# Until the MoE begins: ScalarE's roundings one step later, weight conversion dealt by a table, two buffers for v

## The chip, the cores and the metric

The kernel runs on one core of a Trainium2 chip. The metric is the device time of one execution in microseconds, the median of several runs. The engines are TensorE (PE, matmuls; its weight loads are PEld), VectorE (DVE), ScalarE (ACT), GpSimd (POOL) and the queue of SyncE (SP), which issues nearly all the transfers.

## The reference

Attention with rotary embedding (4 batches, 8 heads, 576 positions, 64 per head), then a feed-forward part that this kernel's names call the MoE, whose hidden layer is gated by a convolution over three neighbouring positions. All of it is float32; the weights come as float64.

```python
q_rot, k_rot = (rotate(q), rotate(k))
scores = scale * np.matmul(q_rot, k_rot.transpose(0, 1, 3, 2))
attn = np.exp(scores - np.max(scores, axis=-1, keepdims=True))
attn = attn / (np.sum(attn, axis=-1, keepdims=True) + 1e-09)
x = np.matmul(attn, v)                  # heads side by side: 576 x 512
h = np.maximum(x @ w_in, 0.0)           # 512 -> 1024
conv_out[s] = sum(conv_w[k] * h[s + k - 1] for k in range(3))
out = (h * sigmoid(conv_out)) @ w_out   # 1024 -> 512
```

## The kernel before

Two heads of a batch make a pair p (16 pairs), and each pair takes five steps: four of 128 query rows for both heads, and a fifth for the remaining 64 rows of both. Step n = 5p + s is thus the unit of the plan. A step holds, for its rows: the scores S (line 260, and line 286 for the last 64 keys), their negated row maximum on VectorE (line 268), the exponential on ScalarE (line 272, into tiles st, or str for a pair's fifth step), and one step later the turning T of the result on TensorE (line 320) and its copy to pt by ScalarE (line 198). Five steps after its first, a pair's pt is multiplied with v (E, line 388; x's half j = 0 and half j = 1). ScalarE copies the product to xn (line 398), VectorE multiplies it with the reciprocal sums that came back by a transfer (line 402, `norm`), ScalarE rounds it to xT (line 406) and GpSimd subtracts the rounded from the exact value (line 407), so that matmuls get x as a high and a low part.

q and k come by six transfers each (lines 148 to 150), GpSimd applies the rotary tables (`rope`: six instructions of line 189 and three of line 192 for a part), and VectorE turns them (line 233 for q, lines 236 to 242 for k). v comes by four transfers into the tiles vm and vr (`load_v`, lines 160 and 161).

For the first 26 steps (`WIDE = 26`) there is no MoE work. In them the 16 weight pieces, 128x512 each, are converted from float64: per piece a transfer (line 587), `first` on ScalarE (line 549), `mid` on VectorE (lines 552, 558 and 561), `third` on VectorE (line 566, which gives wf), and then `split`: ScalarE rounds wf (line 609), and GpSimd subtracts in four quarters (line 612). From step 26 the MoE's units go into the steps: M1 (line 421), its relu on ScalarE into the four tiles rr (line 429), the convolution on VectorE (lines 433 and 435), tanh, gate, rounding, GpSimd's subtraction (line 453) and M2 (lines 503 and 523). The borders of the rr tiles are set to zero by GpSimd (lines 740 and 741) as step 26 begins.

The order on every engine is that in which the code emits. `at(n, rank, fn)` puts a piece of work into step n, in order of rank: 0 T, 0.2 row maxima, 0.3 exponentials, 0.35 the copies that `after` postponed, 0.4 conversion, 0.45 turning of q and k, 0.5 the next step's S, 1.7 and 2.7 `norm`, 2 and 4 further matmuls, 4.5 reciprocals and their transfers, 18 `rope`, 19 loads. `defer(k, fn)` runs fn some ticks later, mostly within the same step. The 48 conversion units are spread evenly over steps 0 to 24.

## Time and profile before

| | us |
|---|---|
| median of 3 runs | 501.51 |
| the runs | 499.65, 501.51, 502.05 |
| the profiled execution, its own time | 499.73 |
| its span, first to last instruction | 497.9 |
| lies around the span | 1.8 |

The trace is read by stretches: the steps without MoE work up to about 123 us, a transition from there to about 187 us, and the rest, in which TensorE carries both attention and MoE. Times are from the span's start. The step of an instruction is found by counting row maxima on VectorE: two in each of a pair's first four steps, one in the fifth.

### The profile page before, as it was taken

The page shows a single profiled execution, that of the slowest core. Times are in us where ns is not written, and L with a number is a line of the kernel's source. Part 1 is how long each engine was busy: PE and PEld are TensorE (multiplying, and loading weights), DVE is VectorE, ACT ScalarE, POOL GpSimd, SP SyncE. Part 2 cuts the span into 40 slices and gives each one's busy share as a digit, 9 for nine tenths or more (in the row PEclk, how much of TensorE's full clock was granted, in tenths as well). Part 3 has the DMA queues.
Part 4 walks back from the last instruction along what each step waited for, and adds up shares of the span by engine and source line. Part 5 has one row for each costly group of instructions (what it writes and reads, how often), then busy time and mean ns, then how long its engine had stood idle before and what let it go on. Part 6 is the DMA issues. An engine that isn't in the chain of part 4 may idle for free.

```text
span 497.9 us, 12391 instructions
## 1 busy us (share of the span) xinstructions
PE 459.4 (92%) x4572; PEld 361.2 (73%) x4572; DVE 357.4 (72%) x643; ACT 327.0 (66%) x927; POOL 300.2 (60%) x479
## 2 busy tenths in 40 slices
PE   1979877787979999999999999999999999999997
PEld 1445554454666869787978787979797978899886
DVE  5689888998394978786868687777674665567921
ACT  2578878777583958686868686868686763234510
POOL 3599997999947666747584849393921213233510
PEclk9989899998897999999999999999999999999999
DMA  8975955755330707070807090707110200100011
GB/s 221 176 137 146 230 129 144 196 113 107 74 69 27 120 9 150 18 149 12 155 19 149 14 153 13 143 25 129 38 48 25 61 12 25 43 22 22 0 65 42
DMA packets 140559, 42.71 MB, mean 86 GB/s; under 512 B 132156, under 2 KB 135252, under 8 KB 140500
## 3 DMA queue, kind: packets, MB, share of 16 engines
q1 hardware_dynamic: 139156, 41.54, 39.9%
q8 instruction: 36, 0.59, 0.5%
q10 hardware_dynamic: 1344, 0.39, 0.4%
q14 instruction: 23, 0.19, 0.1%
HBM read 37.12 MB, written 4.79 MB: 84 GB/s over the span
## 4 chain that ended last, share of the span: by engine, by line
PE 65%; DVE 13%; POOL 7%; DMA 4%; SPq 4%; ACT 3%; issue 2%; DVEq 0%; POOLq 0%; ACTq 0%
PE pm L421 12%; PE sp L260 11%; PE pm L523 10%; PE mt L503 10%; PE pm L388 9%; PE mt L421 7%; PE tp L320 5%; DVE negm L268 4%; POOL rq L189 2%; DMA rq<-q 2%; POOL rk L189 2%; POOL rq L192 2%; DVE wt L558 1%; SPq L149 1%; DVE wt L552 1%
## 5 line engine op out<-in xcount | busy, mean ns | idle before, releaser
L268 DVE TENSOR_REDUCE negm<-sp 128x1 f32<-128x576 f32 x144 | 102.4, 748 | 37.1 <-PE sp L260 28.9
L272 ACT ACTIVATE st<-sp,negm 128x576 f32<-128x576 f32 x128 | 93.8, 740 | 36.7 <-DVE negm L268 35.7
L260 PE MATMUL sp<-kT,qT 64*128 64x288 f32 (+4 forms) x556 | 101.0, 468 | 3.6 <-DVE kT L236 1.6
L453 POOL TENSOR_TENSOR g<-c,g 128x288 fp32r<-128x288 f32 (+4 forms) x88 | 52.5, 618 | 84.6 <-ACT g L452 84.3
L198 ACT ACTIVATE pt<-tp 128x512 f32<-128x512 f32 (+3 forms) x176 | 84.0, 530 | 2.1 <-PE tp L320 1.6
L435 DVE SCALAR_TENSOR_TENSOR c<-rr,cw,c 128x288 f32<-128x288 f32 x128 | 78.4, 612 | 4.5
L421 PE MATMUL pm<-xT,winh 128*128 128x290 f32 x352 | 74.5, 306 | 0.0
L189 POOL TENSOR_TENSOR rq<-rq,tabt 128x192 f32<-128x192 f32 x90 | 58.9, 687 | 16.2 <-DMA rq<-q 16.1
L260 PEld LDWEIGHTS sp<-kT,qT 64*128 64x128 f32 (+1 forms) x556 | 47.5, 178 | 24.8 <-issue 11.1
L407 POOL TENSOR_TENSOR xT<-xn,xT 128x290 fp32r<-128x290 f32 x32 | 27.9, 876 | 61.3 <-ACT xT L406 61.2
L320 PEld LDWEIGHTS tp<-idf,st 64*128 64x128 f32 x1024 | 43.1, 140 | 28.6 <-ACT st L272 18.6
L320 PE MATMUL tp<-idf,st 64*128 64x64 f32 x1024 | 49.4, 229 | 12.7 <-ACT st L272 12.7
L189 POOL TENSOR_TENSOR rk<-rk,tabt 128x192 f32<-128x192 f32 x90 | 57.1, 667 | 5.6 <-DMA rk<-k 5.6
L421 PEld LDWEIGHTS pm<-xT,winh 128*128 128x128 f32 x352 | 56.2, 189 | 1.8
L523 PE MATMUL pm<-wouth,g 64*128 64x256 f32 x576 | 55.5, 282 | 0.0
L388 PE MATMUL pm<-pt,vm 128*64 128x290 f32 x368 | 52.6, 424 | 2.2 <-DMA vm<-v 2.0
L421 PE MATMUL pm<-xT,winl 128*128 128x290 f32 x176 | 52.0, 295 | 0.0
L523 PEld LDWEIGHTS pm<-wouth,g 64*128 64x128 f32 x576 | 48.5, 185 | 0.0
L523 PE MATMUL pm<-woutl,g 64*128 64x256 f32 x288 | 44.0, 277 | 0.0
L433 DVE TENSOR_SCALAR c<-rr,cw 128x288 f32<-128x288 f32 x64 | 28.0, 437 | 21.7 <-ACT rr L429 20.5
L444 DVE SCALAR_TENSOR_TENSOR c<-c,rr 128x288 f32<-128x288 f32 x64 | 35.2, 572 | 9.4 <-ACT c L441 9.4
L388 PEld LDWEIGHTS pm<-pt,vm 128*64 128x64 f32 x368 | 27.2, 142 | 20.1 <-ACT pt L198 2.4
(108 smaller groups left out, 876.6 us busy)
## 6 DMA issues: line engine op xcount, KB each, us to landing
rq<-q SPq DMA_DIRECT2D x30, 144.0 KB
rq<-q SPq DMA_DIRECT2D x60, 72.0 KB
rk<-k SPq DMA_DIRECT2D x30, 144.0 KB
rk<-k SPq DMA_DIRECT2D x60, 72.0 KB
w<-moe_w_in SPq DMA_DIRECT2D x8, 512.0 KB
vm<-v SPq DMA_DIRECT2D x32, 128.0 KB
w<-moe_w_out SPq DMA_DIRECT2D x8, 512.0 KB
rb<-rd SPq DMA_DIRECT2D x16, 144.0 KB
```

Of the source, the lines that this page charges most:

```text
L189: nc.gpsimd.tensor_tensor(out=y, in0=y, in1=tabt[:, a:a + 3], op=ALU.mult)
L198: nc.scalar.activation(out=out, in_=in_, func=AF.Copy, scale=1.0 if sc is None else sc)
L260: nc.tensor.matmul(out=out, lhsT=qt[64 * h:64 * h + 64, c], rhs=kt[64 * h:64 * h + 64, a:a + n], start=True, stop=True)
L268: reds.setdefault((p, s), []).append(lambda: nc.vector.tensor_reduce(out=nm, in_=sc, axis=AX.XY if len(sc.shape) == 3 else AX.X, op=ALU.ma ...
L272: lambda: nc.scalar.activation(out=dst, in_=sc, func=AF.Exp, bias=nm, scale=1.0, accum_out=sm)
L320: nc.tensor.transpose(ps[r][:, 64 * k:64 * k + 64], x[i], idf[i, i])
L388: nc.tensor.matmul(out=xp[64 * h:64 * h + 64, :], lhsT=vmain[p][:, h, i, :] if i < 4 else vrem[:, h, :], rhs=pt[:, 2 * i + h if i < 4 else ...
L421: nc.tensor.matmul(out=ps[:, 0:XW], lhsT=w[:, kk, fs], rhs=xT[:, xs, e, :], start=(i == 0), stop=(i == n - 1))
L435: nc.vector.scalar_tensor_tensor(out=c, in0=r[:, j + e:j + e + HS], scalar=cw[:, 8 * e + f:8 * e + f + 1], in1=c, op0=ALU.mult, op1=ALU.add,)
L453: nc.gpsimd.tensor_tensor(out=lo, in0=c[:, o:o + n], in1=hi.bitcast(F32), op=ALU.subtract)
L503: nc.tensor.matmul(out=ops[tt][:, 0:width], lhsT=g_tile(tt, f, e), rhs=w[:, f, cols], start=(f == 0 and i == 0), stop=(f == NF - 1 and i = ...
L523: nc.tensor.matmul(out=ps[r][:, 0:256], lhsT=g_tile(tt, f, e)[rows], rhs=w[rows, f, cols], start=(f == 0 and i == 0), stop=(f == NF - 1 an ...
```

## The change

There are four edits.

- x's rounding (lines 406 and 407). Before, it ran a tick after `norm`. Now, as long as the next step is below 26, it stands in the next step at rank 0.37: behind that step's exponentials and postponed copies.
- The rounding of a weight piece (lines 609 and 612). Before, it ran two ticks after `third`; now it stands in the next step at rank 0.38.
- The dealing of conversion. Before, equal numbers of units per step; now by the table `ROOM`, one weight for each of a pair's five steps: 1.5, 1.8, 2.5, 0.8, 2.6. The last piece's `mid` moves from step 23 to step 24.
- v. vm and vr have two buffers each, and `load_v(p)` stands in the pair's second step everywhere (before: the fourth, from step 25 on the third). One more memset of vr comes with it, on VectorE in step 6.

```diff
-    vrem = keep.tile([128, 2, D], F32, name="vr")
+    vrem = [keep.tile([128, 2, D], F32, name=f"vr_{s}") for s in range(2)]
...
-        if p == 0:
-            nc.vector.memset(vrem, 0.0)
+        if p < 2:
+            nc.vector.memset(vrem[p], 0.0)
...
-        t = vmain[p] = p1.tile([128, 2, 4, D], F32, tag="vm", name="vm")
+        t = vmain[p] = p1.tile([128, 2, 4, D], F32, tag="vm", name="vm", bufs=2)
...
-        norms[p, j] = lambda: (norm(), defer(1, split))
+        def both():
+            norm()
+            if late["n"] + 1 < WIDE:
+                at(late["n"] + 1, 0.37, split)
+            else:
+                defer(1, split)
+
+        norms[p, j] = both
...
-            defer(2, split)
+            at(late["n"] + 1, 0.38, split)
...
+    ROOM = (1.5, 1.8, 2.5, 0.8, 2.6)
...
-                at(n + (2 if n >= WIDE - 1 else 3), 19, lambda p=p: load_v(p))
+                at(n + 1, 19, lambda p=p: load_v(p))
...
-            nw = len(wsteps)
+            room = [ROOM[x % STEPS] for x in range(WIDE - 1)]
+            ends = [sum(room[:x + 1]) / sum(room) for x in range(WIDE - 1)]
             for i, u in enumerate(wsteps):
-                x = (WIDE - 1) * i // nw
-                at(x, 0.4, u)
+                at(next(x for x, e in enumerate(ends) if (i + 0.5) / len(wsteps) <= e), 0.4, u)
```

VectorE in steps 23 and 24, before. The row maxima x2 are step 23's, the single one is step 24's; w_1345 is the last weight piece, and the xn rows are `norm` of x's two halves:

```order
L268 TENSOR_REDUCE negm<-sp 128x1 x2
L566 SCALAR_TENSOR_TENSOR wf<-w_1235,wt 128x512
L552 TENSOR_SCALAR wt<-wt 128x512
L558 TENSOR_SCALAR wt<-wt 128x512
L561 SCALAR_TENSOR_TENSOR wt<-w_1345,wt 128x512
L236 STREAM_TRANSPOSE kT<-rk 128x576
L240 STREAM_TRANSPOSE kr_89<-rk 64x64 x2
L242 STREAM_TRANSPOSE kT<-rk 128x64
L402 TENSOR_TENSOR xn<-xn,rb 128x290
L268 TENSOR_REDUCE negm<-sp 128x1
L566 SCALAR_TENSOR_TENSOR wf<-w_1345,wt 128x512
L402 TENSOR_TENSOR xn<-xn,rb 128x290
```

The same place after the change, from step 23's turning of k on; w_1295 and w_1349 are the last two pieces:

```order
L236 STREAM_TRANSPOSE kT<-rk 128x576
L240 STREAM_TRANSPOSE kr_90<-rk 64x64 x2
L242 STREAM_TRANSPOSE kT<-rk 128x64
L402 TENSOR_TENSOR xn<-xn,rb 128x290
L268 TENSOR_REDUCE negm<-sp 128x1
L573 SCALAR_TENSOR_TENSOR wf<-w_1295,wt 128x512
L559 TENSOR_SCALAR wt<-wt 128x512
L565 TENSOR_SCALAR wt<-wt 128x512
L568 SCALAR_TENSOR_TENSOR wt<-w_1349,wt 128x512
L573 SCALAR_TENSOR_TENSOR wf<-w_1349,wt 128x512
L402 TENSOR_TENSOR xn<-xn,rb 128x290
L268 TENSOR_REDUCE negm<-sp 128x1 x2
```

The `third` of the last piece but one and the `mid` of the last moved from ahead of step 24's row maximum to behind it, and all five stand now between it and step 25's pair of row maxima.

ScalarE from step 24 to the copy of E's first half (`xn<-tp`), before; str is step 24's exponential, st x2 are step 25's:

```order
L406 ACTIVATE xT<-xn 128x290
L198 ACTIVATE pt<-tp 128x8x64 x2
L272 ACTIVATE str_82,sums<-sp,negm 128x576
L198 ACTIVATE pt<-sp 128x128
L398 ACTIVATE xn<-sp 128x145
L198 ACTIVATE pt<-tp 128x5x64
L198 ACTIVATE pt<-tp 128x4x64
L198 ACTIVATE pt<-tp 64x64
L609 ACTIVATE wouth<-wf 128x512
L272 ACTIVATE st,sums<-sp,negm 128x576 x2
L198 ACTIVATE pt<-sp 128x128
L398 ACTIVATE xn<-tp 128x290
```

And after the change:

```order
L272 ACTIVATE str_83,sums<-sp,negm 128x576
L198 ACTIVATE pt<-sp 128x128
L398 ACTIVATE xn<-sp 128x145
L406 ACTIVATE xT<-xn 128x290
L198 ACTIVATE pt<-tp 128x5x64
L198 ACTIVATE pt<-tp 128x4x64
L198 ACTIVATE pt<-tp 64x64
L272 ACTIVATE st,sums<-sp,negm 128x576 x2
L198 ACTIVATE pt<-sp 128x128
L406 ACTIVATE xT<-xn 128x290
L616 ACTIVATE wouth<-wf 128x512 x2
L398 ACTIVATE xn<-tp 128x290
```

x's rounding went from ahead of step 24's exponential to behind the copy to xn, and x's other half and two weight roundings stand now ahead of the copy of E's first half.

GpSimd from the fifth pair's subtraction of x to the zeroing of the rr borders, before (rk and rq are `rope` of the next pairs):

```order
L189 TENSOR_TENSOR rk<-rk,tabt 128x192 x6
L192 TENSOR_TENSOR rk<-rk 128x6x32 x3
L612 TENSOR_TENSOR woutl<-wf,wouth 128x128 x12
L407 TENSOR_TENSOR xT<-xn,xT 128x290
L189 TENSOR_TENSOR rq<-rq,tabt 128x192 x6
L192 TENSOR_TENSOR rq<-rq 128x6x32 x3
L612 TENSOR_TENSOR woutl<-wf,wouth 128x128 x4
L407 TENSOR_TENSOR xT<-xn,xT 128x290
L189 TENSOR_TENSOR rk<-rk,tabt 128x192 x6
L192 TENSOR_TENSOR rk<-rk 128x6x32 x3
L740 MEMSET rr_1716 128x1
```

And after the change:

```order
L189 TENSOR_TENSOR rk<-rk,tabt 128x192 x6
L192 TENSOR_TENSOR rk<-rk 128x6x32 x3
L619 TENSOR_TENSOR woutl<-wf,wouth 128x128 x8
L407 TENSOR_TENSOR xT<-xn,xT 128x290
L189 TENSOR_TENSOR rq<-rq,tabt 128x192 x6
L192 TENSOR_TENSOR rq<-rq 128x6x32 x3
L407 TENSOR_TENSOR xT<-xn,xT 128x290
L619 TENSOR_TENSOR woutl<-wf,wouth 128x128 x8
L189 TENSOR_TENSOR rk<-rk,tabt 128x192 x6
L192 TENSOR_TENSOR rk<-rk 128x6x32 x3
L747 MEMSET rr_1718 128x1
```

A weight piece's four quarters moved from ahead of `rope` of q to behind it; ahead of the first rk row and ahead of the memset both orders hold the same work.

## Rows read from the trace of the kernel before

**Rows 1.** The page's first line: the span and all instructions.
```profile
span 497.9 us, 12391 instructions
```

**Rows 2.** Busy time by engine in two stretches; columns as the first line says.
```profile
core 0: us, PE busy (x) PEld busy (x) DVE busy (x) ACT busy (x) POOL busy (x), PEclk, DMA share, GB/s
18.00:123.00 105.00, 84.06 (x867) 52.38 (x867) 94.49 (x153) 83.16 (x217) 100.01 (x157) 0.95 0.70 153
...
186.80:498.00 311.20, 307.43 (x3153) 261.04 (x3150) 211.50 (x394) 196.49 (x576) 150.60 (x235) 1.00 0.29 61
```

**Rows 3.** VectorE's waits from 18 to 123.2: total us, times, longest us.
```profile
DVE xn L402 <- ACT xn L398: 3.7, 3, 1.3
DVE wt L552 <- ACT wt L549: 1.5, 1, 1.5
...
DVE kT L236 <- POOL rk L192: 1.0, 1, 1.0
DVE qT L233 <- POOL rq L192: 1.0, 2, 0.5
```

**Rows 4.** GpSimd's waits from 17 to 137, all there are.
```profile
POOL rq L189 <- DMA rq<-q: 7.3, 2, 6.8
POOL xT L407 <- ACT xT L406: 2.7, 1, 2.7
POOL woutl L612 <- ACT wouth L609: 1.8, 1, 1.8
```

**Rows 5.** Timeline of VectorE, steps 23 and 24: start, us, instruction, idle before.
```profile
115.13 0.83 DVE L566 SCALAR_TENSOR_TENSOR wf<-w,wt 128x512 int32<-128x512 int32 x1
...
118.08 0.77 DVE L236 STREAM_TRANSPOSE kT<-rk 128x576 f32<-128x576 f32 x1
...
119.96 0.74 DVE L268 TENSOR_REDUCE negm<-sp 128x1 f32<-128x576 f32 x1
```

**Rows 6.** Timeline of GpSimd from 114: the last ropes and weight quarters.
```profile
114.29 2.13 POOL L192 TENSOR_TENSOR rk<-rk 128x192 f32<-128x192 f32 x3
116.38 6.50 POOL L612 TENSOR_TENSOR woutl<-wf,wouth 128x128 fp32r<-128x128 f32 x12
...
128.74 1.71 POOL L612 TENSOR_TENSOR woutl<-wf,wouth 128x128 fp32r<-128x128 f32 x4
...
136.10 0.10 POOL L740 MEMSET rr<- 128x1 f32 x1
```

**Rows 7.** Timeline of ScalarE, steps 24 to 26.
```profile
120.13 0.45 ACT L406 ACTIVATE xT<-xn 128x290 fp32r<-128x290 f32 x1 [2.41 <-DVE xn L402]
...
123.86 0.63 ACT L609 ACTIVATE wouth<-wf 128x512 fp32r<-128x512 f32 x1
...
127.75 0.41 ACT L398 ACTIVATE xn<-tp 128x290 f32<-128x290 f32 x1 [1.48 <-POOL rq L192]
```

**Rows 8.** Timeline of TensorE: step 26's scores, and E in step 30.
```profile
127.56 1.29 PE L260 MATMUL sp<-kT,qT 64*128 64x288 f32 x8
...
149.37 4.16 PE L388 MATMUL pm<-pt,vm 128*64 128x290 f32 x15 [2.04 <-DMA vm<-v]
```

**Rows 9.** Timeline of VectorE, steps 27 and 28.
```profile
136.34 0.36 DVE L433 TENSOR_SCALAR c<-rr,cw 128x288 f32<-128x288 f32 x1
136.74 1.07 DVE L435 SCALAR_TENSOR_TENSOR c<-rr,cw,c 128x288 f32<-128x288 f32 x2
138.55 1.42 DVE L268 TENSOR_REDUCE negm<-sp 128x1 f32<-128x576 f32 x2 [0.74 <-PE sp L260]
```

**Rows 10.** Busy time in three stretches of E on TensorE, columns as in Rows 2.
```profile
123.40:127.60 4.20, 4.20 (x22) 1.87 (x22) 2.00 (x5) 2.76 (x8) 4.20 (x8) 0.60 0.33 51
131.10:133.80 2.70, 2.70 (x23) 1.41 (x22) 0.00 (x0) 1.40 (x5) 2.70 (x6) 1.00 0.60 115
149.40:155.00 5.60, 5.60 (x23) 3.38 (x25) 1.97 (x3) 0.93 (x4) 5.60 (x10) 0.50 0.03 7
```

**Rows 11.** Timeline of SP's queue, first issue of rk's six and of vm's.
```profile
143.38 0.31 SPq L148 DMA_DIRECT2D rk<-k  x1
...
146.49 0.44 SPq L160 DMA_DIRECT2D vm<-v  x1
```

More of the change, by code (lines that the diff above doesn't have):

```diff
@@ L154, in load_v @@
     def load_v(p):
-        if p == 0:
-            nc.vector.memset(vrem, 0.0)
+        if p < 2:
+            nc.vector.memset(vrem[p], 0.0)
         b, hp = divmod(p, NPB)
-        t = vmain[p] = p1.tile([128, 2, 4, D], F32, tag="vm", name="vm")
+        t = vmain[p] = p1.tile([128, 2, 4, D], F32, tag="vm", name="vm", bufs=2)
         for h in range(2):
             nc.sync.dma_start(out=t[:, h], in_=v[b, 2 * hp + h, 0:512, :].rearrange("(t p) d -> p t d", p=128))
-            nc.sync.dma_start(out=vrem[64 * h:64 * h + 64, h, :], in_=v[b, 2 * hp + h, 512:S, :])
+            nc.sync.dma_start(out=vrem[p % 2][64 * h:64 * h + 64, h, :], in_=v[b, 2 * hp + h, 512:S, :])
     def rope0(part, eng):
@@ L389, in emit_E @@
                     out=xp[64 * h:64 * h + 64, :],
-                    lhsT=vmain[p][:, h, i, :] if i < 4 else vrem[:, h, :],
+                    lhsT=vmain[p][:, h, i, :] if i < 4 else vrem[p % 2][:, h, :],
                     rhs=pt[:, 2 * i + h if i < 4 else 8, o + a:o + a + n],
```

## The prediction

> **What bounds the kernel now.** I read the stretches first. From 186.8 us on TensorE is busy 307.4 of 311.2 us [rows 2], so what another engine saves there is worth nothing; the change can only act by letting that stretch begin earlier. Between 18 and 123 us GpSimd is busy 100.0 and VectorE 94.5 of 105 us, TensorE 84.1 and ScalarE 83.2 [rows 2]: the steps without MoE work are paced by GpSimd and VectorE together. Next I read what these two wait for. VectorE's waits there are few [rows 3]: three times for ScalarE's copy to xn (3.7 us), once for the `first` of the small convolution weights (1.5), twice for q's rope and once for k's (1.0 each). The last belongs to step 3, where GpSimd has worked without a break since its first q landed; nothing changes ahead of that, so it stays. GpSimd waits 5.0 us in all, leaving out its start (7.3 less 6.8, then 2.7 and 1.8) [rows 4]. Last I read steps 23 to 28, where the one regime passes into the other [rows 5 to 10].
>
> **The two anchors.** The end of step 24's row maximum, at 119.96 + 0.74 = 120.70 us, I call A. Behind it the exponential, the turning, E's first half and step 26's scores (127.56) follow each other, and then TensorE's work. The second anchor is step 28's row maximum at 138.55. VectorE reaches it after TensorE's scores, with 0.74 us to spare [rows 9], or after the convolution, which needs the rr borders that GpSimd zeroes at 136.10, behind all its ropes and weight quarters [rows 6]. From 138.55 on nothing in the change alters an order that I see bind, so what 138.55 gains, the end gains.
>
> **Roundings a step later.** No instruction is added. What goes is ScalarE standing still in front of a rounding whose input VectorE has not yet made, 2.41 us in the worst case [rows 7], with the exponential and the copy to xn queued behind; that is what VectorE's three waits for xn come from. Two of them lie ahead of A: 3.7 - 1.3 = 2.4 us. The conversion now dealt to steps 9 and 14 covers them too, and step 12's wait of 1.5 us gets a piece's `mid` and `third` in front of it. q's rope loses a weight piece's quarters ahead of it, so its 1.0 us goes. That is 4.9 us. In step 19 the table leaves VectorE only one `third` between the row maximum and `norm`, so a wait for xn can come up there: nothing to 1.3 us, the longest seen; I take 0.5, since ScalarE no longer stands still first. The added memset of vr has no row of its own; it lies between 0.1 us (a memset on GpSimd, rows 6) and 0.36 (the shortest VectorE row here, rows 9); I take 0.15.
>
> **The table's dealing.** It moves no work off VectorE, but the `third` and `mid` from 115.13 to 118.08 (2.95 us) go behind A [rows 5], where VectorE waits for TensorE anyway. On VectorE alone A would come 2.95 + 4.9 - 0.65 = 7.2 us earlier.
>
> **GpSimd doesn't let it.** The turning of k in step 23 (118.08) needs k's rope, which ended at 114.29 + 2.13 = 116.42, only 1.66 us before. Ahead of that rope the new order holds exactly the same work, so it can come earlier only by waits that GpSimd loses: 2.7 + 1.8 = 4.5 us (the 0.5 for a transfer stays). Against that, two prices. x's subtraction stands ahead of q's rope as before, but its rounding is now behind an exponential and two copies on ScalarE; four such places, each nothing to about 1.3 us (the longest wait for xn, which stems from the same piece of ScalarE's queue, rows 3), so 0 to 5.2; I take 0.8, since where GpSimd runs behind, the rounding is done in time. And GpSimd is slower beside a busy VectorE: a quarter took 6.50 / 12 = 0.54 us at 116.38 with VectorE full, and 1.71 / 4 = 0.43 at 128.74 with it idle [rows 6]. A fifth of 4.9 us of VectorE's waits filled is 1.0 us. So the rope comes 4.5 - 0.8 - 1.0 = 2.7 us earlier, at 113.7, and the turning with it: 118.08 - 113.7 = 4.4. This is less than 7.2, so A gains 4.4 us, set by GpSimd.
>
> The Trainium skill ("SBUF — State Buffer", Who interferes with whom) says that a VectorE instruction with two SBUF inputs contends with a GpSimd instruction that reads SBUF, and that the one that starts second is held for the other's whole length. That speaks against filling VectorE's pauses: by the 0.54 and 0.43 the trace agrees in kind and puts the price at a fifth, and the rule at its full length is the first rival below.
>
> **What the transition takes back.** Behind A VectorE has now five conversion instructions before step 25's row maxima, 2.95 us and one `third` (0.83). Step 26's scores reuse score banks that step 25's exponentials read, so they may come later: 0 to 0.5 us, I take 0.2. On ScalarE two weight roundings (0.63 each, rows 7) stand in front of the copy of E's first half, which frees the bank that step 26's MoE matmuls take; before, that copy followed E directly at 127.75. 0 to 1.3 us; I take 0.6, the part that the exponential's delay doesn't hide. So 4.4 - 0.8 = 3.6 us reach TensorE. The other path into 138.55 gives nearly the same: borders zeroed at 136.10 - 2.7 = 133.4, 0.1 for the memset, then 1.47 for the convolution (136.34 to 137.81), so 134.97 and a gain of at most 3.6.
>
> **v.** In the first steps the loads of v move ahead of q's in SP's queue, but q's load waits there for VectorE's turning, and rope comes later still: nothing. E in step 30 waits 2.04 us for v [rows 8]. Its transfers go out at 146.49 behind k's (143.38), which wait for the turning of step 28 [rows 11]; the new order still has k's six issues ahead of v's four, so I cost this edit at nothing. Weight loads stand later in SP's queue, behind the reciprocals' transfers at steps 15 to 17; each is still issued before ScalarE's `first` takes it, by a step at the least, and ScalarE has 21.8 us free in the 105 [rows 2].
>
> **The sum.** 3.6 us off the profiled execution's 499.73 (its span 497.9 [rows 1] and 1.8 around it) is 496.1. That execution lies 1.8 below the median of the runs shown, so I forecast 501.51 - 3.6 = 497.9.
>
> **The rivals.**
>
> *GpSimd's end does not move.* If every pause that VectorE fills is lost to GpSimd, more than the 4.5 it could save, the rope ends at 116.4 as before. VectorE can then gain 1.66 us at A, and the zeroed borders at 136.2 + 1.47 = 137.67 leave 138.55 - 137.67 = 0.9 us: 500.6. For it: GpSimd was busy in all but 5 us. Against: a quarter is slowed by a fifth, not wholly. This is the skill's lock taken in full.
>
> *The transition loses more than the steps gain (slower).* TensorE's clock falls after standing still: after its 2.04 us wait at 149.37, E's 23 matmuls took 5.60 us at a granted 0.50 (1.2 GHz) where 23 took 2.70 at 1.00 (2.4 GHz) [rows 8, 10]. Before the change E's first half in step 25 ran at 0.60, and step 26's scores followed at once. Now these scores wait for step 25's exponentials, behind VectorE's five conversion instructions. If TensorE stands still there, the matmuls from 127.56 to 133.80, 6.2 us, can run at the lower level: up to 6.2 us more, and 3.4 if about half of them do. With 0.8 for the roundings and only the first rival's 0.9 gained that is 501.51 + 3.4 + 0.8 - 0.9 = 504.8. It decides from the point where A gains less than the 4.2 us that the transition loses. Against: E at 0.60 leaves little room to stand still.
>
> *v's wait goes too.* If the second buffer does free step 30, its 2.04 us go, and E's 23 matmuls run at 2.70 instead of 5.60: 2.0 + 2.9 = 4.9 more, 493.0. Only the queue's order speaks on it, and against.
>
> **How the numbers follow.** The forecast has 0.55, with 495.5 to 499.7 as its own range (a gain of 1.8 to 6: A unbound by GpSimd and no loss in the transition at one end, 2.5 of the waits taken back at the other). GpSimd's end unmoved 0.27, the slower case 0.12, v 0.06. The range 495.3 to 502.4 holds forecast and first rival with a run's spread of about 1.2 either way, and leaves out most of the other two. A measurement of this kernel can tell about 0.5%, 2.5 us, from no change. Faster by more: 0.50 of the forecast and all of v, 0.56. Slower by more: 0.10 of the slower case. Within: 0.27 and what is left of those two, 0.34.
>
> **What would show it.** In the profile after: ScalarE's waits for xn and wf before its roundings gone; VectorE's waits for xn down to one, in step 19; no wait of q's turning for rope; GpSimd's pauses before 123 us under 2 us; k's turning of step 23 starting with its rope's end, near 113.7; A near 116.3; step 28's row maximum near 135, held by the convolution or the scores; v's wait in step 30 unchanged at about 2 us. Wrong: k's turning well after its rope (then VectorE paces), GpSimd's borders still at 136, TensorE at 0.50 between steps 26 and 28, or a wait of ScalarE's `first` for a weight's transfer.

## The result, and the profile after the change

The changed kernel takes 504.37 us (median of 9 executions, 501.42 to 505.43); the kernel before, on the same chip, 500.95 (9 executions, 499.65 to 502.05). The ratio is 1.0055, with a 95% interval of 1.0036 to 1.0075: slower, by about the half per cent that can just be told. The forecast was 497.9, with a range that ended at 502.4. The nine executions fall into two groups, four at 501.4 to 502.5 and five at 504.4 to 505.4 us; the profiled one, 502.03 with a span of 500.3, is of the first, and what sets the second apart came out in the experiments. Medians and counts below are of all executions; ratios and their intervals leave out those that count as slow, over 1.5% above the fastest of the same kernel, some of the long ones of question 3 among them.

First the stretch up to 123 us, by busy time, as in [rows 2] (columns: the stretch, its length, then busy us and instructions of PE, PEld, DVE, ACT and POOL, TensorE's granted clock, DMA share, GB/s). The second row is the stretch of step 26, on which more below:

```profile
18.00:123.00 105.00, 85.16 (x877) 52.33 (x878) 95.35 (x153) 83.26 (x218) 98.26 (x154) 0.92 0.73 156
...
126.80:133.60 6.80, 5.91 (x35) 5.12 (x36) 2.20 (x3) 5.14 (x13) 6.80 (x15) 0.50 0.29 77
```

VectorE and GpSimd are as busy as before (95.35 and 98.26 against 94.49 and 100.01). The waits from 17 to 123 us show what was exchanged for what (engine, tile and line that waited, what it waited for: us in total, times, longest). VectorE's:

```profile
DVE negm L268 <- PE sp L388: 4.3, 4, 2.1
...
DVE xn L402 <- ACT xn L398: 0.6, 1, 0.6
```

GpSimd's:

```profile
POOL winl L619 <- ACT winh L616: 3.2, 3, 1.3
POOL winl L619 <- DVE wt L559: 2.4, 1, 2.4
POOL xT L407 <- ACT xT L406: 1.1, 3, 0.7
```

And two of ScalarE's:

```profile
ACT wt L556 <- DMA w<-moe_w_in: 3.6, 1, 3.6
ACT wt L556 <- DMA w<-moe_w_out: 2.2, 2, 1.9
```

What the change set out to remove is gone: ScalarE's waits for xn and wf ahead of its roundings, VectorE's for the small weights' `first`, and two of VectorE's three waits for xn [rows 3]. In their place stand waits of VectorE's row maxima for TensorE (4.3 us), two rows of GpSimd ahead of weight quarters (3.2 and 2.4), and two rows of ScalarE's `first` (line 556 now) for a weight's transfer (3.6 and 2.2), which did not exist before. VectorE's timeline around A and behind it (start us, us, engine, line, operation, out<-in, count, the idle time before and what ended it); k's turning and step 24's row maximum stood at 118.08 and 119.96 [rows 5]:

```profile
117.39 0.77 DVE L236 STREAM_TRANSPOSE kT<-rk 128x576 f32<-128x576 f32 x1
...
119.06 0.75 DVE L268 TENSOR_REDUCE negm<-sp 128x1 f32<-128x576 f32 x1
...
124.47 1.41 DVE L268 TENSOR_REDUCE negm<-sp 128x1 f32<-128x576 f32 x2
...
137.77 1.42 DVE L268 TENSOR_REDUCE negm<-sp 128x1 f32<-128x576 f32 x2 [6.31 <-PE sp L260]
139.10 0.36 DVE L440 TENSOR_SCALAR c<-rr,cw 128x288 f32<-128x288 f32 x1
...
141.31 1.42 DVE L268 TENSOR_REDUCE negm<-sp 128x1 f32<-128x576 f32 x2 [0.30 <-PE sp L260]
```

A gained 0.9 us and not 4.4. Behind it, five conversion instructions and `norm` hold step 25's row maxima until 124.47 (123.11 before), and ScalarE's exponentials wait 3.68 us for them. Step 26's scores on TensorE:

```profile
127.69 1.80 PE L260 MATMUL sp<-kT,qT 64*128 64x288 f32 x5 [2.57 <-ACT pt L198]
```

TensorE stood 2.57 us before the rest of step 26's scores, and the granted clock from 126.8 to 133.6 was 0.50, which is 1.2 GHz, where before it was back at 1.00 (2.4 GHz) by 131.1 [rows 10]. The rest of the scores came at nearly the time at which all eight had begun before (127.69 against 127.56), so the 0.9 us gained at A were gone; step 26 then lasted 8.70 us instead of 6.12, and step 28's row maximum came 2.76 late (141.31 against 138.55 [rows 9]). From there on the two traces run 2.6 us apart to the end. So in this execution the loss is step 26 at half speed, and the small gain ahead of it is spent before that step. Other executions of the same order lose their time elsewhere (question 3).

### The profile page after: what moved, and what is told of

Same layout as the page of the kernel before. It is cut to its first block, busy times and chain, and to the rows that moved or that the text cites. A ratio compares the mean times of both kernels' runs of the same rounds, so it can differ in the third digit from the quotient of the medians.

```text
span 500.3 us, 12391 instructions
## 1 busy us (share of the span) xinstructions
PE 460.5 (92%) x4572; PEld 362.7 (73%) x4572; DVE 360.0 (72%) x644; ACT 326.7 (65%) x927; POOL 299.9 (60%) x479
## 4 chain that ended last, share of the span: by engine, by line
PE 75%; DMA 8%; DVE 8%; SPq 2%; ACT 2%; POOL 2%; issue 1%; DVEq 0%; POOLq 0%; ACTq 0%
PE pm L428 15%; PE sp L260 14%; PE pm L388 12%; PE pm L530 10%; PE mt L510 10%; PE mt L428 7%; PE tp L320 6%; DMA w<-moe_w_out 3%; DVE negm L268 2%; DMA w<-moe_w_in 1%; DMA rq<-q 1%; ACT st L272 1%; DMA rb<-rd 1%; POOL rq L189 1%; DVE wt L568 1%
## 5 line engine op out<-in xcount | busy, mean ns | idle before, releaser
L260 PE MATMUL sp<-kT,qT 64*128 64x288 f32 (+4 forms) x556 | 103.8, 475 | 4.0 <-ACT pt L198 2.6
L428 PE MATMUL pm<-xT,winh 128*128 128x290 f32 x352 | 75.6, 309 | 0.0
L189 POOL TENSOR_TENSOR rq<-rq,tabt 128x192 f32<-128x192 f32 x90 | 61.3, 713 | 16.7 <-DMA rq<-q 16.2
```

The costliest lines, as they stand in the source:

```text
L189: nc.gpsimd.tensor_tensor(out=y, in0=y, in1=tabt[:, a:a + 3], op=ALU.mult)
L260: nc.tensor.matmul(out=out, lhsT=qt[64 * h:64 * h + 64, c], rhs=kt[64 * h:64 * h + 64, a:a + n], start=True, stop=True)
L428: nc.tensor.matmul(out=ps[:, 0:XW], lhsT=w[:, kk, fs], rhs=xT[:, xs, e, :], start=(i == 0), stop=(i == n - 1))
```

## Experiments

18 runs, each timed beside the kernel before on the same chip (`r1` and `r2` are one execution each). Line numbers of kernels with added lines are higher by that number. A "held" execution is explained at the third question; I count times of 504 us and more.

### 1. Does the transition cost what TensorE's standing still costs?

`e4_filler`: the changed kernel with TensorE kept busy in step 25.

```diff
+            filler["ps"] = t_tile()
+            return filler["ps"][:, 0:n]
...
+    FILL = 7
...
+        if "m" not in psum and late["n"] + 1 == WIDE:
+            for _ in range(FILL):
+                nc.tensor.matmul(
+                    out=filler["ps"][:, 320:512], lhsT=idf, rhs=pt[:, 0, 0:192], start=True, stop=True
+                )
```

> The changed kernel with seven matmuls added on TensorE in step 25, behind E's first half, whose results nobody reads; they fill the 2.57 us in which TensorE stands before step 26's scores (about 0.4 us each by the 0.49 of the two on line 286). The output stays as it is. If the fall of the clock in steps 26 and 27 comes from that standing, the granted clock there is 1.00, the matmuls of steps 26 from the scores to E's second half take 3 us less, and the time falls to about 501.3. Rival (the clock falls for the waits before, in step 24, or of itself): clock 0.5 in the same place, time as the changed kernel or up to 0.5 us longer.

Measured: 500.94, ratio 1.0026 (0.9996 to 1.0056); eight of twelve at or under 502.3, four over 504. TensorE's timeline behind E's first half:

```profile
124.67 2.54 PE L400 MATMUL tp<-pt,idf 128*128 128x192 f32 x14
127.14 1.24 PE L263 MATMUL sp<-kT,qT 64*128 64x288 f32 x8
```

And two stretches of the same kernel by busy time and clock (columns as above):

```profile
120.70:124.10 3.40, 3.40 (x18) 1.73 (x16) 3.30 (x5) 0.14 (x1) 3.40 (x5) 0.50 0.30 46
124.10:131.00 6.90, 6.90 (x62) 5.65 (x60) 3.20 (x7) 5.19 (x14) 6.90 (x15) 1.00 0.13 43
```

All eight score matmuls go in one piece at 2.4 GHz, step 26 takes 6.14 us, and the profiled time is 500.14 instead of 502.03; the eight executions without the times over 504 have a median of 500.3, where the four such of the changed kernel have 502.0, which speaks for the added matmuls. That step 26 at the low clock is the loss of that profile is read directly from its rows. That the standing still brings the clock down is not shown by `e4`, whose low clock lies in E's first half: `e1`, `e7` and `e9` have it there too, at 0.60 to 0.63 from 120.6 to 124.9 us, without the added matmuls, and then 1.00 in step 26. In `r1` TensorE stood 1.94 us before the scores, and the clock stayed at 1.00 (its scores, and the stretch of step 26):

```profile
126.97 0.99 PE L260 MATMUL sp<-kT,qT 64*128 64x288 f32 x5 [1.94 <-ACT pt L198]
...
126.80:133.60 6.80, 6.63 (x59) 4.78 (x61) 2.11 (x3) 4.91 (x13) 6.80 (x15) 1.00 0.48 108
```

So where the low clock falls differs between executions of one order, and what decides it stays open. The standing still by itself, at the full clock, makes step 26 6.75 us long instead of 6.12 in `r1`.

`e2_last_as_before`: the changed kernel, its last four conversion units back in their old steps. `e1_loads_early`: the changed kernel, each weight load issued a piece earlier. `e3_both`: both edits.

```diff
-                at(next(x for x, e in enumerate(ends) if (i + 0.5) / len(wsteps) <= e), 0.4, u)
+                x = next(x for x, e in enumerate(ends) if (i + 0.5) / len(wsteps) <= e)
+                if i >= len(wsteps) - 4:
+                    x = (WIDE - 1) * i // len(wsteps)
+                at(x, 0.4, u)
...
-            load_w(i + 3)
+            load_w(i + 4)
...
             load_w(2)
+            load_w(3)
```

> The changed kernel, with the last four conversion units in the steps where the kernel before has them (22, 23, 23, 24 instead of 23 and three times 24), so that VectorE has one conversion instruction instead of five between the row maxima of steps 24 and 25. My theory: those five hold step 25's exponentials, these hold step 26's scores (TensorE stood 2.57 us), and the clock's fall to 1.2 GHz from 126.8 to 133.7 follows from that standing. Then the scores follow E within 0.5 us, the granted clock is 1.00 over steps 26 and 27, step 26 takes 6.1 instead of 8.7 us, the row maximum of step 24 comes up to 3 us later, and the time is about 1 us lower, 503.4. Rival (what was moved behind step 24's row maximum is the gain, and the clock falls anyway): 3 us slower, 507.

> The changed kernel, with every weight piece's load issued one piece earlier (four at the start, then piece i+4 behind piece i). My theory: in the changed kernel ScalarE stands 3.6 us in step 4 to 5 for piece 3's transfer, which went out at 31.3 us behind q's six issues instead of at 21.7, and the row maximum of step 7 comes at 45.5 us instead of 42.7 for it. With the load back at the start that wait goes, step 7 begins at 42.7 or before, and the time falls by 2.8 us, 504.4 to about 501.6. Rival (GpSimd paces, so ScalarE's standing costs nothing in the end): step 7 earlier, step 24's row maximum still near 119, time within 1 us of the changed kernel.

> Both edits of the two kernels before this one. My theory: the two causes lie in different steps and add up: 504.4 - 2.8 - 1.0, about 500.6, which is the kernel before within 0.3%. Rival (only one of them is on the path): the better of the two alone.

Measured: `e2` 503.3 (ratio 1.0062, six of twelve over 504), `e1` 504.73 (1.0066, four of seven over 504) and `e3` 500.99 (1.0032, 1.0001 to 1.0063; four of twelve over 504). In `e2` and `e3` step 26's scores follow E at once and the step takes 6.13 and 6.14 us, as expected. In `e1` ScalarE's waits for weights are gone, and step 24's row maximum is at 118.1; but `e1` missed its 501.6, the 503.3 of `e2` is the middle between two groups (six at 500.3 to 501.9, six at 504.8 to 507.6) and meets its 503.4 by luck, and the profiled executions of `e1` and `e2`, 505.15 and 507.18, showed something that no theory had.

### 2. Which part of the change carries which loss?

`p1_roundings` is the kernel before with x's and the weights' roundings a step later and nothing else; `p2_room` with the table's dealing alone; `p3_v` with v's two buffers and its earlier loads alone. Their edits are the three parts of the change's diff.

> The kernel before with the roundings' part of the change alone: x's and the weights' roundings a step later, the conversion's steps, the weight loads and v as before. Prediction's theory: VectorE's and GpSimd's waits go, step 24's row maximum comes 2 to 3 us earlier and the time with it, 497.5 to 498.5. What the changed kernel's trace makes me believe now: GpSimd's 4.5 us of waits are replaced by others, since a quarter a step later is missing in GpSimd's queue while it has nothing else (2.4 us and 3.2 us ahead of quarters in the changed kernel), so step 24's row maximum moves by under 1 us; time 500 to 501, with an upper group if GpSimd's borders end after 137.8.

> The kernel before with only the dealing of conversion by the table of room. My theory: it carries both the weight loads that stand later in SP's queue and the conversion behind step 24's row maximum, so ScalarE waits for weight transfers and TensorE stands still before step 26's scores; lower group 501 to 502.5, some executions above 504. Rival (the later roundings carry the loss): 500.5.

> The kernel before with only the two buffers of v and its earlier loads. Prediction and theory agree: v's wait in step 30 stays near 2 us, because k's transfers stand ahead of v's in SP's queue; 500.5, within 0.2% of before. Rival of the prediction (the second buffer frees step 30): 496.

Measured: `p1` 504.98, eight of twelve over 504, ratio 1.0038 (1.0005 to 1.007); its profiled execution took 501.08. `p2` 501.77, none over 504, ratio 1.0016 (0.9992 to 1.0041). `p3` 500.32, one of twelve over 504, ratio 0.9981 (0.9954 to 1.0008). First the waits of `p1` from 17 to 123 us, VectorE's:

```profile
DVE qT L233 <- POOL rq L192: 2.1, 2, 1.6
DVE xn L402 <- ACT xn L398: 1.8, 3, 0.6
DVE negm L268 <- PE sp L286: 1.3, 1, 1.3
DVE negm L268 <- PE sp L388: 1.3, 1, 1.3
DVE wt L559 <- ACT wt L556: 1.2, 1, 1.2
DVE kT L236 <- POOL rk L192: 1.0, 1, 1.0
```

GpSimd's:

```profile
POOL rq L189 <- DMA rq<-q: 7.2, 1, 7.2
POOL winl L619 <- ACT winh L616: 3.9, 2, 1.9
POOL xT L407 <- ACT xT L406: 2.3, 2, 2.0
POOL xT L407 <- DMA rk<-k: 0.7, 1, 0.7
```

VectorE's waits add up to 8.7 us, and to 8.8 before (7.2 in [rows 3], beside 1.3 for scores and 0.3 for a transfer); GpSimd's to 14.1, and to 11.8 before [rows 4]. The later roundings shorten the waits for xn (3.7 to 1.8) and bring as much elsewhere. As I read the rows, GpSimd's quarters, a step later, are missing from its queue while it has nothing else (3.9 us ahead of them), and then stand in front of a rope (2.1 us of VectorE's for q's). Step 24's row maximum in `p1` is at 120.85: no gain, since the five traces that keep the old roundings and the old dealing up to there (`before`, `e6`, `e8`, and but for v's loads `p3` and `b7`) have it at 119.96 to 121.04. In `p2` it is at 117.24, 2.7 earlier than in `before`, and other rows of `p2` name the price. ScalarE's wait in front of `first`, from its waits up to 123 us:

```profile
ACT wt L549 <- DMA w<-moe_w_in: 3.5, 1, 3.5
```

Step 24's row maximum in VectorE's timeline:

```profile
117.24 0.74 DVE L268 TENSOR_REDUCE negm<-sp 128x1 f32<-128x576 f32 x1
```

Step 26's scores on TensorE:

```profile
126.19 1.78 PE L260 MATMUL sp<-kT,qT 64*128 64x288 f32 x5 [2.25 <-ACT pt L198]
```

So the table alone brings, at A, nearly the 2.95 us of moved conversion, and loses them behind A, where TensorE stands still and step 26 takes 9.10 us (granted clock 0.54 from 126.8 to 133.6). `p3` keeps the wait for v, 2.42 us where 2.04 was before [rows 8]; TensorE's timeline:

```profile
151.16 1.38 PE L388 MATMUL pm<-pt,vm 128*64 128x290 f32 x4 [2.42 <-DMA vm<-v]
```

### 3. What are the executions over 504 us?

`r1_after` is the changed kernel again, to see such an execution; it was one, at 506.74 us. VectorE's timeline at the first convolution, which took 0.36 us before [rows 9] and in the first profile after:

```profile
137.25 5.30 DVE L440 TENSOR_SCALAR c<-rr,cw 128x288 f32<-128x288 f32 x1 [1.30 <-POOL rr L747]
```

GpSimd's, from the last border on:

```profile
137.35 0.10 POOL L748 MEMSET rr<- 128x1 f32 x1
137.40 3.36 POOL L189 TENSOR_TENSOR rq<-rq,tabt 128x192 f32<-128x192 f32 x6
140.72 1.67 POOL L192 TENSOR_TENSOR rq<-rq 128x192 f32<-128x192 f32 x3
```

VectorE's instruction begins beside GpSimd's zeroing and ends when GpSimd's nine rope instructions end, which follow the zeroing without a pause. Step 28's row maximum, ScalarE and TensorE stand behind it, and the last row maximum comes 4.7 us later than in the first profile (408.80 against 404.09). Before the change GpSimd had a pause right there: it zeroed the borders at 136.10 [rows 6] and then waited 1.35 us for q's transfer, and in that pause the convolution ran.

> The changed kernel again, to see an execution of its upper group if this one is one: then, by my theory, its first convolution takes 5.3 us behind GpSimd's zeroing and step 27 about 8.5 us; if it lies in the lower group, at 501.4 to 502.5, it takes 0.4 and step 27 3.5.

`e6_before_quarters_twice` provokes it in the kernel before: 1.7 us more GpSimd work, so that q has landed when the borders are zeroed.

```diff
-                for o in range(0, 512, 128):
+                for o in list(range(0, 512, 128)) * (2 if i == len(WPIECES) - 1 else 1):
```

> The kernel before, with the four weight quarters of the last piece done twice on GpSimd (the same values again, 4 x 0.43 = 1.7 us more), so that its zeroing of rr's borders ends near 137.9 us, when q has just landed (137.79 before), and q's rope follows without a pause. My theory of the hold: executions at 504 to 506 us appear in the kernel before too, and where the profile has one, the first convolution takes about 5.3 us. Where it is not held, borders at 138.1 plus 1.47 of convolution put the row maximum of step 28 at 139.6, 1.0 later than 138.55: 501.5. Rival (no hold, only the later borders): all executions at 500.5 to 502.

Measured: 504.44, ratio 1.006 (1.0037 to 1.0083), six of ten over 504 and two more at 503.8 and 503.9. VectorE's timeline in its profile:

```profile
138.01 5.31 DVE L433 TENSOR_SCALAR c<-rr,cw 128x288 f32<-128x288 f32 x1 [1.11 <-POOL rr L740]
```

GpSimd's:

```profile
138.16 3.37 POOL L189 TENSOR_TENSOR rq<-rq,tabt 128x192 f32<-128x192 f32 x6
```

Two edits to find what is held. `e5_borders_vector` (and `r2_borders_vector`, the same once more): VectorE zeroes the borders itself. `e7_two_inputs` and `e8_quarters_two_inputs`: the convolution's first instruction with two tensors as inputs, in the changed kernel and in `e6`.

```diff
...
-                        nc.gpsimd.memset(t[:, 0:1], 0.0)
-                        nc.gpsimd.memset(t[:, XW:XW + 1], 0.0)
+                    at(WIDE + 1, 0.25, borders)
...
-            nc.vector.tensor_scalar(out=c, in0=r[:, j:j + HS], scalar1=cw[:, f:f + 1], scalar2=None, op0=ALU.mult)
+            nc.vector.scalar_tensor_tensor(
+                out=c, in0=r[:, j:j + HS], scalar=cw[:, f:f + 1], in1=zero, op0=ALU.mult, op1=ALU.add
+            )
```

> The changed kernel with one thing moved: VectorE zeroes the eight border columns of rr itself, directly ahead of its first convolution in step 27, so that convolution waits for nothing of GpSimd. My theory: the executions of the changed kernel at 504.4 to 505.4 us are those in which that convolution (5.3 us where 0.36 is usual) is held until GpSimd, which goes from the zeroing into q's rope without a pause, has ended all nine rope instructions. Without the wait all executions lie in the lower group, 501 to 502.6, median about 502.0 (the memsets cost VectorE under 0.5 us). Rival (the upper group comes from somewhere else, such as the clock): still two groups, median near 504, and step 27 or a later step long again.

> The changed kernel with VectorE's own borders again, five of twelve executions of which lay at 504.5 us or above, to see one of these. My theory: a VectorE instruction with one tensor as input is held there too for several us, at the first or second convolution, beside q's rope. Rival: no VectorE instruction is longer than usual, and the time is lost elsewhere, which the trace then names.

> The changed kernel with the first of the three convolution instructions in another form: the same product with a tensor of zeros added, so that it has two tensors as inputs like the two behind it, instead of one. In all traces so far only the form with one tensor was held for 5.3 us. My theory (the upper group of times is that hold, wherever it falls): no executions at 504 to 506 us, median 501.5 to 502.5, the lower group of the changed kernel. Rival (the upper group has another cause, which the kernel with VectorE's own borders hinted at with five of twelve above 504): two groups as before, median near 504.

> The kernel before with the last piece's quarters done twice, eight of ten executions of which lay at 503.8 to 505.5 with the first convolution held for 5.31 us, and now the convolution's first instruction with two tensors as inputs. My theory: not held, 0.5 to 0.9 us instead of 5.31, and all executions at 500.4 to 502. Rival (any VectorE instruction that comes between GpSimd's borders and its rope is held): again a first convolution of 5 us and a median near 504.5.

Measured: `e5` 501.68 (ratio 1.0012), still five of twelve over 504; `r2` 505.28; `e7` 503.68 (1.0066), three of eight over 504 (none under 502.2); `e8` 505.97 (1.0092), seven of ten. Both theories fell, the wait for the borders and the instruction's form, as these rows show; three executions, 510.47 (`e5`), 510.77 (`e7`) and 513.92 (`e8`), lie higher still, and no trace has one. VectorE's timeline in `r2`:

```profile
135.65 6.20 DVE L440 TENSOR_SCALAR c<-rr,cw 128x288 f32<-128x288 f32 x1
```

GpSimd's in `r2`:

```profile
135.04 1.70 POOL L192 TENSOR_TENSOR rk<-rk 128x192 f32<-128x192 f32 x3
136.71 3.34 POOL L189 TENSOR_TENSOR rq<-rq,tabt 128x192 f32<-128x192 f32 x6
140.02 1.66 POOL L192 TENSOR_TENSOR rq<-rq 128x192 f32<-128x192 f32 x3
```

VectorE's in `e7`:

```profile
136.66 5.48 DVE L441 SCALAR_TENSOR_TENSOR c<-rr,cw,zero 128x288 f32<-128x288 f32 x1 [0.76 <-POOL rr L750]
```

In `r2` the convolution waits for nothing of GpSimd, and is held still longer: from inside k's rope to the end of q's. What the held executions have in common is GpSimd's unbroken run of instructions. But such a run is not enough: in the profiles of `p1`, `e3`, `e4` and `e5` q's rope followed too within 0.11 us, and the convolution took 0.37 to 0.54 us. There GpSimd paid a little instead, its six instructions taking 3.86 to 4.11 us where they took 3.34 to 3.37 beside a held convolution. In `p1`, VectorE's convolution and GpSimd's rope:

```profile
138.12 0.37 DVE L440 TENSOR_SCALAR c<-rr,cw 128x288 f32<-128x288 f32 x1 [1.03 <-POOL rr L747]
138.25 4.11 POOL L189 TENSOR_TENSOR rq<-rq,tabt 128x192 f32<-128x192 f32 x6
```

`e9_pause`: the changed kernel, with q's rope of step 27 put behind the first convolution by one small copy on GpSimd that reads its output.

```diff
+        late.setdefault("c0", c)
...
+            at(27, 17, lambda: nc.gpsimd.tensor_copy(mark, late["c0"][:, 0:1]))
```

> The changed kernel with one GpSimd copy of a single column ahead of q's rope of step 27, which reads what the first convolution wrote, so that the rope waits for it and GpSimd makes a pause there, as it did before the change (1.35 us for q's transfer). My theory: the first convolution takes 0.4 to 0.6 us in all executions, none lies above 504 us, and the median is that of the changed kernel's lower group, 501.4 to 502.5. Rival (the two groups come from elsewhere and the hold only accompanies them): executions at 504 to 507 stay, about half.

Measured: 501.95 (498.99 to 503.93), ratio 1.0007 (0.998 to 1.0034), none of twelve over 504. VectorE's timeline:

```profile
136.26 0.37 DVE L442 TENSOR_SCALAR c<-rr,cw 128x288 f32<-128x288 f32 x1 [0.75 <-POOL rr L750]
```

GpSimd's copy, which waits for the convolution:

```profile
137.80 0.18 POOL L725 COPY mark<-c 128x1 f32<-128x1 f32 x1 [1.34 <-DVE c L444]
```

The pause alone takes the times over 504 away, and with them the measurable slowdown. Over the 18 profiled executions (all but those of the last two experiments below) the line is clean: the seven in which the first convolution was held took 504.85 to 507.18 us, the eleven others 498.99 to 502.22.

Six of these have the changed kernel's order up to step 26, and side by side they show what the two groups of its times are (us; the clock is that granted from 126.8 to 133.6):

| | TensorE's wait before step 26's scores | clock | step 26 | first convolution | time |
|---|---|---|---|---|---|
| `after` | 2.57 | 0.50 | 8.70 | 0.36 | 502.03 |
| `e5` | 2.62 | 0.75 | 8.02 | 0.54 | 500.61 |
| `r1` | 1.94 | 1.00 | 6.75 | 5.30 | 506.74 |
| `r2` | 1.95 | 1.00 | 6.76 | 6.20 | 505.28 |
| `e7` | 0.92 | 1.00 | 6.77 | 5.48 | 505.21 |
| `e9`, with the pause | 0.91 | 1.00 | 6.75 | 0.37 | 498.99 |

The changed kernel paid in one place or the other. Where step 26 ran at the low clock, the convolution came late, inside q's rope, and was not held. Where the clock stayed up, it began beside k's rope or the zeroing, ahead of q's rope, and without the pause it was held. Only `e9`'s profile has neither loss. For the executions without a profile this is inferred from their times.

### 4. Is there a version that beats both?

`b1_both_borders_vector` (`e3` with VectorE's borders) and `b5_early_filler_pause` (`e1`, `e4` and `e9` together).

> The changed kernel with all three causes taken out: weight loads a piece earlier, the last four conversion units in their old steps, and the borders zeroed by VectorE. My theory: no upper group (the same kernel with GpSimd's borders had four of twelve executions at 505.7 to 506.1), all executions near its lower group, 499.6 to 501.1, so the median is 500.3, the same as before within 0.2%. Rival (the gain upstream was only hidden by GpSimd's borders): 498 to 499.

> The changed kernel with all three losses taken out and the conversion left where the change deals it: weight loads a piece earlier, seven matmuls nobody reads on TensorE in step 25 against its standing still, and GpSimd's pause. My theory: step 24's row maximum at 118.1, step 28's near 137.0 against 138.5 before, no upper group, so 499.0 (498.3 to 500.0), 0.3% below before. Rival (step 28 is held by GpSimd's zeroed borders or by the rope put later): 500.5.

Measured: `b1` 500.32, ratio 1.0011 (0.998 to 1.0041), three of twelve over 504. `b5` 500.4, ratio 0.9993 (0.9969 to 1.0017), none over 504. With all three losses addressed, `b5` only equals the kernel before, though its step 28 has its row maximum at 137.10, 1.45 earlier. One of k's issues took 1.70 us instead of 0.50 there, v left at 146.67 behind it (146.49 before [rows 11]), and E in step 30 waited for v. SP's queue in `b5`:

```profile
142.92 1.70 SPq L154 DMA_DIRECT2D rk<-k  x1
...
146.67 0.38 SPq L164 DMA_DIRECT2D vm<-v  x1
```

TensorE's timeline in `b5`:

```profile
149.69 1.84 PE L392 MATMUL pm<-pt,vm 128*64 128x290 f32 x5 [3.32 <-DMA vm<-v]
```

In this execution, then, v's late landing took back what step 28 had gained; in `e9`'s profile, step 28 0.9 earlier, 0.7 passed to the end (span 497.3 against 497.9). `b6_v_ahead` (on `b5`) and `b7_before_v_ahead` (on `p3`) put v's issues ahead of q's and k's, which two buffers allow.

```diff
-                at(n + 1, 19, lambda p=p: load_v(p))
+                at(n if n >= WIDE - 1 else n + 1, 18.5 if n >= WIDE - 1 else 19, lambda p=p: load_v(p))
```

> The kernel b5 (loads a piece earlier, matmuls nobody reads, GpSimd's pause) with v's four issues ahead of q's and k's in SP's queue from step 25 on, which its two buffers allow. My theory: v lands before 136 us, E of step 30 begins when its weights are turned, near 146.4 instead of 149.69, at 2.4 GHz, so that 23 matmuls take 2.7 instead of 5.6; 3.3 + up to 2.9 off 500.4: 494 to 497.5. Rival: q, now behind v, lands 2.3 us later, its rope and turning hold a later step, and 499 to 501 is left.

> The kernel before with v's two buffers and v's four issues ahead of q's and k's in SP's queue from step 25 on; nothing else of the change. My theory: E of step 30 loses its wait of 2.04 us and the clock at 1.2 GHz behind it, 2.0 + 2.9 = 4.9 at most, and 2.0 at least: 495.6 to 498.5. Rival: as for b6, q's later landing gives it back, 500 to 501.

Measured: 514.03 (ratio 1.0254, 1.022 to 1.0288) and 512.14 (1.0214, 1.0179 to 1.0248). That is the rival of both, and more. TensorE's timeline in `b6`, where E begins:

```profile
147.01 2.17 PE L392 MATMUL pm<-pt,vm 128*64 128x290 f32 x16
```

GpSimd's, at q's rope:

```profile
171.23 3.67 POOL L193 TENSOR_TENSOR rq<-rq,tabt 128x192 f32<-128x192 f32 x6 [9.64 <-DMA rq<-q]
```

VectorE's, at k's turning:

```profile
183.58 0.78 DVE L240 STREAM_TRANSPOSE kT<-rk 128x576 f32<-128x576 f32 x1 [5.71 <-POOL rk L196]
```

v's wait is gone and E runs at once. But q's load is now behind v's, GpSimd waits 9.64 us for it, and k's rope and turning come too late for the next pair's first scores: each such step is 1.2 to 3.2 us longer from then on (steps 36 to 79 take 230.1 us instead of 219.0). v between q and k was not tried.

## Why the prediction was wrong, step by step

- **Roundings, 4.9 us of VectorE's waits and 4.5 of GpSimd's: wrong.** Most of the waits named in the forecast did go; q's turning kept half of its 1.0 us, and step 19 keeps 0.6 us for xn where it took 0.5. But other waits took their place, one for one: alone, this part gains nothing at A (`p1`). In the profile after, k's rope of step 23 ends at 115.7 and not at 113.7, and the turning follows only at 117.39, so VectorE paced there, which the forecast named as a sign against it. The step treated a removed wait as time won, without asking what the engine meets next. Its price for GpSimd beside VectorE rests on a misread row: at 128.74 VectorE was not idle, its two row maxima ran from 128.88 on:

```profile
128.88 1.42 DVE L268 TENSOR_REDUCE negm<-sp 128x1 f32<-128x576 f32 x2 [3.41 <-PE sp L260]
```

  GpSimd's end of "2.7 us earlier" falls with it: its borders were zeroed 1.1 us later in the profile after (137.24) and 1.8 later in `p1`.
- **The table's dealing, 2.95 us: right upstream.** `p2` gains 2.7 at A. A in the changed kernel gained 0.9 to 2.3 in the seven profiled executions that have its order up to there (`after`, `r1`, `e5`, `r2`, `e7`, `e9`, `e4`).
- **Weight loads later in SP's queue, costed at nothing: wrong.** The sentence held that each load is issued before `first` takes it; what counts is when it has landed. In the profile after, ScalarE stood in front of `first` for it, with pt's copy queued behind. The load's issue in SP's queue:

```profile
31.27 0.98 SPq L594 DMA_DIRECT2D w<-moe_w_in  x2
```

  And the `first` that takes it, in ScalarE's timeline:

```profile
37.46 0.66 ACT L556 ACTIVATE wt<-w 128x512 f32<-128x512 f32 x1 [3.56 <-DMA w<-moe_w_in]
```

  Issued a piece earlier, with the rest of the order up to there kept, step 24's row maximum came at 118.1, 117.3 and 118.0 (`e1`, `b5`, `b6`). The seven have it at 117.7 to 119.1, so the wait is shown, but a price of it at A is not clear of their spread.
- **The transition, 0.8 us: mis-sized.** The scores' delay (0.2) was a wait of 2.57 in the profile after, and step 26 took 2.6 us longer, 2.0 of it by the low clock (8.70 against 6.75 in `r1`). In this execution it is the slower rival by its mechanism, and its condition holds: A gained less than the transition lost. But the clock falls there in only two of the six executions of the table; in the other four the wait is 0.91 to 1.95 and step 26 is 0.6 us longer, at the full clock. "E at 0.60 leaves little room" was wrong: in `after`, `r1`, `e5` and `r2` E's first half ran at 1.00. That standing still brings the clock down, which the rival took from E in step 30, is likely here and not shown: waits of 2.57 and 2.62 us, and of 2.25 in `p2`, were followed by the low clock, 1.94 and 1.95 were not.
- **GpSimd and the convolution: missing.** The forecast followed the borders to the convolution and asked only when they are zeroed, and not what stands behind them in GpSimd's queue. Five of nine executions of the changed kernel lay over 504, and 3 of 135 of the kernel before in all comparisons. This hold, and not the rival's clock, is what the executions over 504 and so the median of 504.37 show; that the rival's 504.8 lies near it is luck. `p1` has eight of twelve over 504, `p2` none, so it comes mostly with the roundings, which end GpSimd's run ahead of the rope after q has landed (`e6` brings it on in the kernel before by that alone).
- **v at nothing: right** (`p3`). The rival "v's wait goes too" did not come: the second buffer leaves the wait in place. Where another edit removes it, the kernel is 11 us slower (`b7`) and not 4.9 faster.
- **"What 138.55 gains, the end gains": wrong.** The 1.45 us of `b5` are gone at the end, which v's late landing took back; of the 0.9 of `e9`, 0.7 arrive.

What stays open: where the low clock falls in an execution, why an unbroken run of GpSimd holds the convolution in some executions and not in others, why only this first one, and the three times over 510.

## What to carry to other kernels

A wait that is removed from an engine near its limit is a gain only if the trace shows that the engine has something ready in its place; in `p1` 8.8 us of VectorE's waits became 8.7 of others. When an order moves, follow each load from its issue to its landing, and each instruction that frees another engine to what comes right behind it in its own queue. Before a pause is closed, look for what lived on it: here VectorE's turn beside GpSimd. And where times of one program fall into groups, profile several executions: one profile showed only one of the two losses.

## What the runs showed of the hardware

A VectorE instruction of 0.36 us (0.5 in its form with two inputs) took 5.30 to 6.20 us in seven profiled executions, while GpSimd ran nine to eleven rope instructions without a pause beside it; it ended only when that run ended. The Trainium skill ("SBUF — State Buffer", Who interferes with whom) says that the engine that issues first has the shared ports for the whole instruction and that the other is blocked for it. By that rule the wait would be one GpSimd instruction, by estimate 3.36 / 6 = 0.56 us (`r1`); measured were nine and more in a row, so the measurement goes further than the Trainium skill. That section of the Trainium skill counts `tensor_scalar` in its two-port mode and instructions with two SBUF inputs among those that can contend; both forms were held here, 5.30 us with one tensor input (`r1`) and 5.48 with two (`e7`). On the other hand some 4,070 other VectorE instructions with one or two tensor inputs (TENSOR_SCALAR, SCALAR_TENSOR_TENSOR, TENSOR_TENSOR) began beside a running GpSimd instruction in the 20 traces and took 1.5 us at most, which the Trainium skill's rule would allow. What decides between the two no run here shows. With a pause of GpSimd none of 24 executions (`e9` and `b5`) took over 504 us, and in the two that were profiled the convolution took 0.37.
